# Attention with a compressive memory and a two-matrix MLP on one core: the gate and the pairs of keys and values move from GpSimd to ScalarE and VectorE

## The chip, the core and the metric

The kernel runs on one core of one Trainium2 chip. A core has TensorE (PE in the profile: matmuls; PEld is its weight load), VectorE (DVE), ScalarE (ACT), GpSimd (POOL) and SyncE (SP, which issues the DMAs). The metric is device time in microseconds (us), lower is better: 618.44 us for the kernel before, the median of 3 runs (617.84 to 619.04).

## The reference, cut to what matters

```python
def _attn_ref(q, k, v, M_prev, z_prev, beta):          # B, H, S, D = 4, 8, 576, 64
    scores = scale * np.matmul(q, k.transpose(0, 1, 3, 2))
    scores = np.where(causal, -1e9, scores); scores = scores - scores.max(-1, keepdims=True)
    a = np.exp(scores); a /= a.sum(-1, keepdims=True) + 1e-09
    local = np.matmul(a, v)
    q_p = phi(q)                                        # where(x > 0, x, exp(x) - 1) + 1
    mem_ret = np.einsum('bhsd,bhde->bhse', q_p, M_prev)
    mem_norm = np.einsum('bhsd,bhd->bhs', q_p, z_prev)[..., None] + 1e-06
    g = 1.0 / (1.0 + np.exp(-beta))[None, :, None, None]
    return g * mem_ret / mem_norm + (1 - g) * local

def _moe_ref(x, w_in, w_out, alpha):                    # x: 2304 x 512, w_in: 512 x 2048, w_out: 2048 x 512
    h = x @ w_in
    g = np.maximum(h, 0.0) + alpha * np.minimum(h, 0.0)
    return (g @ w_out).astype(np.float32)
```

The rows of the attention, with the heads side by side, are the x of the MLP. The inputs are float32, with the MLP's weights read as pairs of 32-bit words.

## The kernel before, in words

**Pairs of halves.** Nearly every matmul operand x is kept as two float16 tiles, hi = half(s·x) and lo = half(s·x − hi), where s is a power of two found from the data; a product is then three matmuls (hi·hi, hi·lo, lo·hi). Three engines make such a pair in one of two ways. The long way: GpSimd multiplies x by s in place (`tensor_tensor`), ScalarE copies the product to float16 (a CAST in the profile), GpSimd subtracts (`tensor_tensor`) to get lo. The scaled way: ScalarE writes hi in one `activation` with scale s, VectorE writes lo in one `scalar_tensor_tensor`, (x·s) − hi.

**Stages.** The first 64 rows of all four batches are computed together (called Z, batch number 4 in the names), the other 512 rows batch by batch in two groups of 256 rows (block pairs [1, 2] and [3, 4]). A unit is one head of such a group: scores in PSUM (tile `s`), mask and row minimum on VectorE (`E<-s,mask`), exponential on ScalarE, the sums' reciprocals (`sm`), the pair of probabilities (`P<-E,sm` on ScalarE and `P<-E,sm,P` on VectorE), a DMA transpose (`PT<-P`) and the product with the values (`bank<-v,PT`, then the pair `xn` and its transpose into `x`). Units follow each other with a lag of 3 between scores and values.

**MLP steps.** There are 9 groups of 256 rows with 8 steps each, 72 steps in all. `moe_in` does 24 matmuls `h<-x,R` for 256 hidden columns, then `r<-h` (ScalarE), two `r<-r,oma,h` (VectorE), and makes the pair `gg` of the gate; `moe_out`, one step later, does 12 matmuls `y<-R,gg`. The table `GL` says for which half groups the gate's pair is made the long way: 7 half groups of 4 steps, so 28 of the 72 steps; of the others 16 have a constant as the scale (the two groups that are done while the weights still come in) and 28 use the scaled way with the scale `gsc`.

**Weights.** `load_w` brings a piece of 128 x 1024 weights as pairs of words, `conv_w` makes float32 of it on VectorE (three instructions `R<-…` per piece: one `tensor_scalar`, two `scalar_tensor_tensor`), and `split_w` makes the float16 pair in the tile R; its last step is on GpSimd (`R<-R`, 16 times). The 16 pieces are the main work of the first 110 us.

**Keys and values.** For each batch b from 1 on and each of 4 pairs of heads hp, `build_qk` makes the pair `k<-kn` (128 x 640) and sends it to a DMA transpose; for every b and hp, `build_v` makes the pair `v<-vn` (128 x 640), where block 0 (128 columns, half of it the memory M) has a scale of its own (`pm`), and blocks 1 to 4 (512 columns) the scale `scr`. `KS` and `VS` pick the engine of the first multiplication: GpSimd for all values and for the keys of batches 1 and 2, ScalarE for the keys of batch 3.

**Order of the work.** All operations are first recorded (class `Work`, so nearly every instruction has line 272 in the profile) and then laid out by a list planner with prices per operation (`price`, `lag`, `lay`, `issue`). The table `STAGES` adds a bias in microseconds to the due time of each phase (such as "bv0" for `build_v` of batch 0, "LW2" for loads of weights, "y1_10" for steps of a group, "P:POOL" for one engine's part). Each engine then runs its own list in that order; SyncE's list orders the DMAs.

Of the kernel before, what the change touches and what calls it, by code (L numbers as in the profile page):

```python
# [18 lines left out]
KS = [1, 1, 1, 0]  # L19
VS = [1, 1, 1, 1]  # L20
QL = [0, 0, 0, 0]
GL = [0, 0, 0, 0, 1, 1, 1, 1, 1, 1, 1, 0, 0, 0, 0, 0, 0, 0]
# [12 lines left out]
        "A0": 60.3, "A:DVE": -306.4, "BK0": 117.9, "BK:PE": -11.5, "C0": 4, "C1": -76.9, "C2": -1.6, "C3": 79.3,  # L35
        "C:ACT": -0.6, "C:DVE": -39.3, "C:PE": -397.4, "I": -157.5, "I:DVE": -330.7, "J": 263.4, "J:ACT":
# [8 lines left out]
        -50.1, "P:PE": -496.3, "P:POOL": 679, "S1": 1377.4, "S2": -9, "S3": -27.5, "S:ACT": -46, "S:POOL": 29.2,  # L45
# [7 lines left out]
        "o:DMA": 27.6, "o:DVE": 63.6, "o:PE": 10.9, "oZ": -65.4, "oZ:DVE": 37.9, "oZ:POOL": 3, "p0": -58, "p1":  # L53
        334.1, "p2": -935.6, "p3": 1.5, "p:ACT": 144.4, "p:DVE": 12.4, "p:POOL": 37.5, "q1": 25.3, "q2": 66.4,
        "q:ACT": -27.9, "q:DVE": -643.9, "r0": -38.4, "r:ACT": 109.4, "r:DVE": -26.1, "r:POOL": -14, "s03": 7.2,
        "s11": -466, "s13": -162.8, "s21": -1.8, "s23": 262.8, "s31": -144.7, "s33": -269.1, "s:ACT": -108.2,
# [219 lines left out]
def kernel(  # L276
# [120 lines left out]
    def load_batch(b):  # L397
# [3 lines left out]
        if b:  # L401
            kr = natp.tile([128, NS, H, D], F32, tag="kn")
        else:
            kr = stack["v16"].rearrange("p (i h d) -> p i h d", i=NS, d=D)
# [832 lines left out]
```

## Time and profile before

| | |
|---|---|
| median of 3 runs | 618.44 us (617.84 to 619.04) |
| the profiled execution's own time | 617.69 us |
| its span on the core | 615.9 us, mean granted clock of TensorE 0.953 |
| busy: PE / DVE / ACT / POOL | 534.2 / 467.4 / 378.9 / 268.9 us |
| share of the chain that ended last | PE 49%, DVE 31%, DMA 5%, ACT 5% |

The span is cut into stretches in the rows below: the start (to 120 us, of which 20 to 40 is shown; weights and the first attention), a stretch in which VectorE is busy nearly all the time (120 to 300), a stretch with PE nearly full (300 to 500) and the tail (from 500), where the attention has ended and PE runs MLP steps alone. A busy time is a union, so instructions of one engine that overlap at their ends count once; the idle time of an engine is the stretch less its busy time.

### The profile page before, as it was taken

Reading aid. Unit: us, or ns where it says so; the run is one execution under the profiler, and the core shown is the slowest. Engines: PE = TensorE matmul, PEld = TensorE weight load, DVE = VectorE, ACT = ScalarE, POOL = GpSimd, SP = SyncE. Lnnn points to the kernel's source line nnn. Section 1 sums busy time; section 2 is a strip of 40 time slices with the busy share of each in tenths; the row PEclk is TensorE's granted clock in tenths of the full one; section 3 lists DMA queues with packets and bytes.
Section 4 is the critical chain, followed back from the end, with each engine's and each line's share of the span. In section 5 each row is a group of like instructions: output and inputs, shape, how many; then the busy total and the mean of one; then the engine's idle time right before and its main releaser. Section 6 shows DMA issues by size and latency. Waiting matters only on the chain.

```text
span 615.9 us, 12153 instructions
## 1 busy us (share of the span) xinstructions
PE 534.2 (87%) x4450; PEld 354.1 (57%) x4450; DVE 467.4 (76%) x1118; ACT 378.9 (62%) x795; POOL 268.9 (44%) x255
## 2 busy tenths in 40 slices
PE   0525567998989989898999999799999999999997
PEld 0314444545545666654666676557667666776773
DVE  5599999889889899999978555878757867733322
ACT  2536577566977856686785556748678757732322
POOL 2137254466297751565455545987553511000000
PEclk9966768899999999998999999999999999999999
DMA  8975879312935999865998390249776536610000
GB/s 277 189 256 190 239 227 219 81 32 51 186 87 108 188 205 173 180 151 122 208 196 180 67 167 35 53 87 196 167 161 115 100 81 147 129 40 19 35 1 35
DMA packets 228060, 82.87 MB, mean 135 GB/s; under 512 B 218272, under 2 KB 218272, under 8 KB 228000
## 3 DMA queue, kind: packets, MB, share of 16 engines
q1 hardware_dynamic: 228000, 82.09, 60.5%
q8 instruction: 35, 0.57, 0.4%
q14 instruction: 25, 0.20, 0.1%
HBM read 35.66 MB, written 5.77 MB: 67 GB/s over the span
## 4 chain that ended last, share of the span: by engine, by line
PE 49%; DVE 31%; DMA 5%; ACT 5%; issue 4%; SPq 3%; POOL 2%; DVEq 0%; ACTq 0%; POOLq 0%
PE y L272 20%; PE h L272 17%; PE s L272 7%; DVE R L272 6%; DVE P L272 5%; PE bank L272 4%; DVE q L272 4%; DVE E L272 3%; SPq L272 3%; DVE r L272 3%; DMA PT<-P 2%; DVE sm L272 2%; DVE gg L272 2%; ACT E L272 1%; ACT P L272 1%
## 5 line engine op out<-in xcount | busy, mean ns | idle before, releaser
L272 PE MATMUL h<-x,R 128*128 128x256 f16 x1728 | 286.3, 279 | 19.3 <-DVE r L272 10.3
L272 PE MATMUL y<-R,gg 128*128 128x512 f16 x864 | 247.0, 383 | 4.8 <-DVE gg L272 4.0
L272 PEld LDWEIGHTS <-R 128*128 128x128 f16 x1728 | 170.9, 100 | 69.3 <-issue 22.7
L272 PE MATMUL bank<-v,PT 128*128 128x64 f16 x1224 | 190.8, 193 | 6.4 <-DVE xn L272 4.0
L272 PEld LDWEIGHTS <-gg 128*128 128x128 f16 x864 | 84.7, 99 | 90.2 <-issue 6.5
L272 PEld LDWEIGHTS <-PT 128*128 128x128 f16 x1224 | 117.8, 98 | 13.0 <-issue 6.3
L272 DVE SCALAR_TENSOR_TENSOR P<-E,sm,P 128x320 f16<-128x320 f32 (+2 forms) x112 | 85.7, 790 | 20.3 <-ACT P L272 19.7
L272 DVE SCALAR_TENSOR_TENSOR r<-r,oma,h 128x256 f32<-128x256 f32 x144 | 62.8, 474 | 38.7 <-ACT r L272 38.5
L272 ACT ACTIVATE E<-E,mx 128x448 f32<-128x448 f32 (+2 forms) x112 | 69.9, 624 | 32.3 <-DVE mx L272 31.8
L272 ACT ACTIVATE P<-E,sm 128x320 f16<-128x320 f32 (+2 forms) x112 | 65.3, 621 | 23.4 <-DVE sm L272 14.8
L272 ACT ACTIVATE r<-h 128x512 f32<-128x512 f32 x72 | 42.3, 592 | 55.3 <-PE h L272 45.1
L272 PE MATMUL s<-k,qT 128*128 128x192 f16 (+7 forms) x200 | 66.9, 375 | 4.7 <-DVE mx L272 3.9
L272 POOL TENSOR_TENSOR P<-q,P 128x128 f16<-128x128 f32 x56 | 31.0, 554 | 91.1 <-ACT P L272 87.5
L272 DVE CUSTOM_DVE_ANT_0 E<-s,mask,pm 128x320 f32<-128x320 f32 (+3 forms) x96 | 56.5, 610 | 9.6 <-PE s L272 8.5
L272 POOL TENSOR_TENSOR R<-R 128x1024 f16<-128x1024 f32 x16 | 36.7, 2296 | 19.0 <-ACT R L272 19.0
L272 POOL TENSOR_TENSOR gg<-r,gg 128x512 f16<-128x512 f32 x28 | 34.9, 1248 | 19.7 <-ACT gg L272 14.3
L272 POOL TENSOR_TENSOR r<-r,gsc 128x512 f32<-128x512 f32 x28 | 31.9, 1143 | 21.8 <-DVE sm L272 7.3
L272 DVE SCALAR_TENSOR_TENSOR gg<-r,gsc,gg 128x512 f16<-128x512 f32 x28 | 22.9, 819 | 16.8 <-ACT gg L272 16.7
L272 PE MATMUL s<-k,qS 128*128 128x192 f16 (+3 forms) x120 | 33.9, 294 | 0.0
L272 ACT ACTIVATE gg<-r,gsc 128x512 f16<-128x512 f32 x28 | 20.1, 719 | 20.3 <-PE y L272 12.5
L272 DVE SCALAR_TENSOR_TENSOR sm<-sm,C 128x2 f32<-128x2 f32 x64 | 23.2, 363 | 12.3 <-ACT E L272 10.9
L272 POOL TENSOR_TENSOR t<-q,zb 128x512 f32<-128x512 f32 x16 | 23.2, 1456 | 19.6 <-DVE wsc L272 12.2
(178 smaller groups left out, 745.1 us busy)
## 6 DMA issues: line engine op xcount, KB each, us to landing
q<-in_q_dram SPq DMA_DIRECT2D x16, 256.0 KB, 4.9
vn<-in_v_dram SPq DMA_DIRECT2D x16, 256.0 KB, 4.8
out_dram<-t SPq DMA_DIRECT2D x16, 256.0 KB, 2.3
kn<-in_moe_w_in_dram SPq DMA_DIRECT2D x6, 512.0 KB, 5.2
kn<-in_moe_w_out_dram SPq DMA_DIRECT2D x6, 512.0 KB, 5.5
kn<-in_k_dram SPq DMA_DIRECT2D x12, 256.0 KB, 3.8
qS<-qT SPq DMA_DIRECT2D x24, 128.0 KB, 2.4
R<-in_moe_w_in_dram SPq DMA_DIRECT2D x4, 512.0 KB, 7.5
```

The costliest lines, as they stand in the source:

```text
L272: fn(*a, **kw)
```

## The change

The long way goes for the gate, the keys and the values; all of them use the scaled way. `KS` and `VS` go, `GL` is all zeros. The value pair is made in two pieces (block 0; blocks 1 to 4), each with an activation and a `scalar_tensor_tensor`. For batches from 1 on the keys lie as [head, block, column] in SBUF so that a pair of heads can be addressed in one piece; before they lay as [block, head, column]. `STAGES` gets another set of biases (some 240 numbers), and with it the planner lays out all lists anew.

```diff
-KS = [1, 1, 1, 0]
-VS = [1, 1, 1, 1]
-GL = [0, 0, 0, 0, 1, 1, 1, 1, 1, 1, 1, 0, 0, 0, 0, 0, 0, 0]
+GL = [0] * 18
...
 STAGES = [
     (2, {
-        "A0": 60.3, "A:DVE": -306.4, "BK0": 117.9, "BK:PE": -11.5, "C0": 4, "C1": -76.9, "C2": -1.6, "C3": 79.3,
+        "A0": 31.3, "A:DVE": 38.7, "BK0": -19.6, "BK:ACT": -1.3, "BK:PE": 157.4, "C0": -144.5, "C1": 360.2,
...
         if b:
-            kr = natp.tile([128, NS, H, D], F32, tag="kn")
+            kn = kr = natp.tile([128, H, NS, D], F32, tag="kn")
         else:
             kr = stack["v16"].rearrange("p (i h d) -> p i h d", i=NS, d=D)
+            kn = kr.rearrange("p i h d -> p h i d")
         vn = natp.tile([128, H, NS, D], F32, tag="vn")
-        kn = kr.rearrange("p i h d -> p h i d")
...
-        V.tensor_reduce(t[:, 1:2], nat[b]["kr"].rearrange("p i h d -> p (i h d)"), **ab)
+        V.tensor_reduce(t[:, 1:2], nat[b]["kr"].rearrange("p h i d -> p (h i d)"), **ab)
...
-        kk = n["k"][:, hs]
-        kh, kl = (k16[:, :, :, t, :] for t in range(2))
-        if KS[b]:
-            G.tensor_tensor(kk, kk, p["sk"][:, :, None, None].to_broadcast([128, 2, NS, D]), op=ALU.mult)
-        else:
-            A.activation(kk, kk, AF.Copy, scale=p["sk"])
-        A.copy(kh, kk)
-        G.tensor_tensor(kl, kk, kh, op=ALU.subtract)
+        kk = n["k"][:, hs].rearrange("p h i d -> p (h i) d")
+        kh, kl = (k16[:, :, :, t, :].rearrange("p h i d -> p (h i) d") for t in range(2))
+        A.activation(kh, kk, AF.Copy, scale=p["sk"])
+        V.scalar_tensor_tensor(out=kl, in0=kk, scalar=p["sk"], in1=kh, op0=ALU.mult, op1=ALU.subtract)
...
         for i0, i1, sc in ((0, 1, p["sv0"]), (1, NS, p["sv"])):
-            vv = n["v"][:, hs, i0:i1].rearrange("p h i d -> p h (i d)")
-            if VS[b]:
-                G.tensor_tensor(vv, vv, sc[:, :, None].to_broadcast([128, 2, (i1 - i0) * D]), op=ALU.mult)
-            else:
-                A.activation(vv, vv, AF.Copy, scale=sc)
-        vv = n["v"][:, hs].rearrange("p h i d -> p h (i d)")
-        vh, vl = (v16[:, t].rearrange("p h i d -> p h (i d)") for t in range(2))
-        A.copy(vh, vv)
-        G.tensor_tensor(vl, vv, vh, op=ALU.subtract)
+            vv, vh, vl = (x[:, :, i0:i1].rearrange("p h i d -> p h (i d)") for x in (n["v"][:, hs], v16[:, 0], v16[:, 1]))
+            A.activation(vh, vv, AF.Copy, scale=sc)
+            V.scalar_tensor_tensor(out=vl, in0=vv, scalar=sc, in1=vh, op0=ALU.mult, op1=ALU.subtract)
```

**How the lists move, place 1: VectorE at the start**, from the last instruction on alpha's scale on (`isa`). `stq`, `q<-q,t` and `zmx` belong to Z's attention and wait for Z's loads; `R<-kn` and `R<-R` convert weights, here the first pieces of w_out. Before:

```order
L272 TENSOR_SCALAR isa<-scr_100 128x1
L272 TENSOR_REDUCE stq_104<-q_0_91 128x1 x2
L272 SCALAR_TENSOR_TENSOR q_0_91<-q_0_91,t_0_133 128x512
L272 TENSOR_SCALAR str_106<-stq_104 128x2
L272 RECIPROCAL str_106<-str_106 128x2
L272 SCALAR_TENSOR_TENSOR q_0_91<-q_0_91,t_1_134 128x512
L272 ISA P_108,zmx_117<-s_0_116,mz 128x64
```

The same place in the change:

```order
L272 TENSOR_SCALAR isa<-scr_100 128x1
L272 TENSOR_SCALAR R<-kn_88 128x1024
L272 SCALAR_TENSOR_TENSOR R<-kn_88,R 128x1024
L272 TENSOR_REDUCE stq_104<-q_0_91 128x1
L272 SCALAR_TENSOR_TENSOR R<-kn_88,R 128x1024
L272 SCALAR_TENSOR_TENSOR q_0_91<-q_0_91,t_0_133 128x512
L272 TENSOR_SCALAR R<-R 128x1024
L272 SCALAR_TENSOR_TENSOR R<-R 128x1024
L272 TENSOR_REDUCE stq_104<-q_0_91 128x1
L272 SCALAR_TENSOR_TENSOR R<-R 128x1024
L272 SCALAR_TENSOR_TENSOR q_0_91<-q_0_91,t_1_134 128x512
```

Two whole pieces of weights now stand between the instructions of Z; the first `zmx` stands behind the 9th converted piece, where it stood behind the 4th.

**Place 2: VectorE at the first MLP step** (`r<-r,oma,h` is the step's first work on VectorE; `mx` with the mask is a score of batch 0). Before:

```order
L272 SCALAR_TENSOR_TENSOR R<-E_0_90,R 128x1024
L272 SCALAR_TENSOR_TENSOR R<-kn_88,R 128x1024
L272 SCALAR_TENSOR_TENSOR R<-E_0_90,R 128x1024
L272 SCALAR_TENSOR_TENSOR r_144<-r_144,oma,h_112 128x256
L272 TENSOR_REDUCE stq_105<-q_2_93 128x1 x2
```

In the change:

```order
L272 TENSOR_SCALAR R<-q_0_89 128x1024
L272 ISA P_108,mx_148<-s_0_121,mask 128x320
L272 ISA mx_148 128x1
L272 ISA P_108,mx_148<-s_0_121,mask 128x192
L272 SCALAR_TENSOR_TENSOR r_144<-r_144,oma,h_112 128x256 x2
L272 SCALAR_TENSOR_TENSOR r_145<-r_145,oma,h_113 128x256 x2
```

The `r` of the first two steps stand together behind 14 converted pieces and the first scores of batch 0, where the first stood behind 12 pieces and no such score.

**Place 3: the long way on GpSimd and what stands for it on VectorE**, in the middle of the program. GpSimd before, in batch 2 (`P<-q,P` is the part of a unit that stays there):

```order
L272 TENSOR_TENSOR r_144<-r_144,gsc 128x512
L272 TENSOR_TENSOR P_108<-q_1_92,P_108 128x2x64
L272 TENSOR_TENSOR r_145<-r_145,gsc 128x512
L272 TENSOR_TENSOR P_109<-q_1_92,P_109 128x2x64
L272 TENSOR_TENSOR v_66<-vn_95,v_66 128x640
L272 TENSOR_TENSOR gg_146<-r_144,gg_146 128x512
```

VectorE in the change, at the keys of batch 2:

```order
L272 SCALAR_TENSOR_TENSOR gg_146<-r_144,gsc,gg_146 128x512
L272 SCALAR_TENSOR_TENSOR q_0_89<-q_3_94,scr_101,q_0_89 128x8x64
L272 SCALAR_TENSOR_TENSOR sm_151<-sm_151,C_131 128x2
L272 SCALAR_TENSOR_TENSOR xn_161<-bank_67,xsc,xn_161 128x256
L272 SCALAR_TENSOR_TENSOR k_0_110<-kn_88,scr_101,k_0_110 128x10x64
L272 RECIPROCAL sm_151<-sm_151 128x2
```

The gate's and the keys' splits now stand in VectorE's list between the instructions of the units, and GpSimd's list keeps `P<-q,P`, the norms (`t<-q,zb`, `q<-q,nrm`) and the weights (`R<-R`).

## Rows read from the trace of the kernel before

**Rows 1.** Busy time by engine in stretches: PE, PEld, DVE, ACT, POOL, clock, DMA
```profile
core 0: us, PE busy (x) PEld busy (x) DVE busy (x) ACT busy (x) POOL busy (x), PEclk, DMA share, GB/s
20.00:40.00 20.00, 10.73 (x83) 7.68 (x83) 12.22 (x56) 7.47 (x14) 4.62 (x4) 0.91 1.00 254
120.00:300.00 180.00, 166.31 (x1284) 102.46 (x1283) 167.42 (x409) 127.36 (x268) 100.28 (x88) 0.98 0.68 136
300.00:500.00 200.00, 193.24 (x1811) 131.74 (x1810) 148.03 (x375) 137.22 (x324) 117.61 (x119) 1.00 0.64 128
500.00:616.00 116.00, 112.17 (x989) 76.79 (x985) 50.55 (x110) 47.79 (x88) 3.94 (x6) 1.00 0.28 62
```

**Rows 2.** Waits of PE from 120 to 300: total us, times, longest
```profile
PE h L272 <- DVE r L272: 4.8, 3, 2.8
PE y L272 <- DVE gg L272: 4.0, 3, 2.2
```

**Rows 3.** Timeline of VectorE, 20 to 26 us: start, us, what, idle before
```profile
23.82 0.69 DVE L272 TENSOR_REDUCE stq<-q 128x1 f32<-128x512 f32 x1 [3.27 <-DMA q<-in_q_dram]
```

**Rows 4.** Groups by form, VectorE, whole span: the conversion of weights
```profile
L272 DVE SCALAR_TENSOR_TENSOR R<-kn,R 128x1024 int32<-128x1024 int32 x10 | 12.1, 1214 | 0.1
...
L272 DVE TENSOR_SCALAR R<-kn 128x1024 int32<-128x1024 int32 x5 | 3.6, 722 | 5.1 <-DMA kn<-in_moe_w_in_dram 5.1
```

**Rows 5.** Timelines of GpSimd and of VectorE at 304 us
```profile
304.57 1.42 POOL L272 TENSOR_TENSOR r<-r,gsc 128x512 f32<-128x512 f32 x1
305.02 1.52 DVE L272 SCALAR_TENSOR_TENSOR gg<-r,gsc,gg 128x512 f16<-128x512 f32 x1
```

**Rows 6.** Groups by form, VectorE, 500 to 616 us: xcount, busy us, mean ns
```profile
L272 DVE SCALAR_TENSOR_TENSOR gg<-r,gsc,gg 128x512 f16<-128x512 f32 x20 | 15.0, 751 | 16.8 <-ACT gg L272 16.7
L272 DVE SCALAR_TENSOR_TENSOR P<-E,sm,P 128x576 f16<-128x576 f32 x6 | 4.9, 816 | 1.8 <-ACT P L272 1.8
```

**Rows 7.** Groups by form, VectorE, 120 to 300 us
```profile
L272 DVE SCALAR_TENSOR_TENSOR P<-E,sm,P 128x576 f16<-128x576 f32 x12 | 12.7, 1059 | 2.0 <-ACT P L272 2.0
...
L272 DVE SCALAR_TENSOR_TENSOR sm<-sm,C 128x2 f32<-128x2 f32 x23 | 12.1, 530 | 1.1 <-ACT E L272 0.7 <-ACT P L272 0.4
...
L272 DVE SCALAR_TENSOR_TENSOR q<-q,scr,q 128x512 f16<-128x512 f32 x8 | 10.7, 1363 | 0.0
```

**Rows 8.** Groups by form, VectorE, 300 to 500 us
```profile
L272 DVE SCALAR_TENSOR_TENSOR P<-E,sm,P 128x576 f16<-128x576 f32 x14 | 15.2, 1083 | 4.8 <-ACT P L272 4.5
...
L272 DVE SCALAR_TENSOR_TENSOR P<-E,sm,P 128x320 f16<-128x320 f32 x16 | 12.9, 805 | 8.6 <-ACT P L272 8.3 <-issue 0.2
...
L272 DVE SCALAR_TENSOR_TENSOR sm<-sm,C 128x2 f32<-128x2 f32 x31 | 7.9, 255 | 8.7 <-ACT E L272 8.6
```

**Rows 9.** Groups by form, GpSimd, 120 to 300 us
```profile
L272 POOL TENSOR_TENSOR R<-R 128x1024 f16<-128x1024 f32 x8 | 17.0, 2129 | 7.6 <-ACT R L272 7.6
...
L272 POOL TENSOR_TENSOR k<-kn,k 128x640 f16<-128x640 f32 x8 | 13.3, 1666 | 10.6 <-ACT k L272 10.6
L272 POOL TENSOR_TENSOR t<-q,zb 128x512 f32<-128x512 f32 x8 | 11.8, 1480 | 6.0 <-DVE q L272 6.0
L272 POOL TENSOR_TENSOR P<-q,P 128x128 f16<-128x128 f32 x20 | 11.7, 585 | 36.4 <-ACT P L272 34.8 <-DMA qS<-qT 1.5
L272 POOL TENSOR_TENSOR v<-vn,v 128x640 f16<-128x640 f32 x8 | 11.4, 1444 | 3.5 <-ACT v L272 3.5
```

**Rows 10.** Groups by form, GpSimd, 300 to 500 us
```profile
L272 POOL TENSOR_TENSOR gg<-r,gg 128x512 f16<-128x512 f32 x28 | 34.9, 1248 | 19.7 <-ACT gg L272 14.3 <-PE s L272 2.2 <-PE h L272 1.9
...
L272 POOL TENSOR_TENSOR P<-q,P 128x128 f16<-128x128 f32 x30 | 15.3, 513 | 21.6 <-ACT P L272 19.5 <-PE h L272 2.0
```

**Rows 11.** Groups by form, ScalarE, whole span
```profile
L272 ACT ACTIVATE gg<-r,gsc 128x512 f16<-128x512 f32 x28 | 20.1, 719 | 20.3 <-PE y L272 12.5 <-DVE r L272 7.6
L272 ACT CAST gg<-r 128x512 f16<-128x512 f32 x28 | 17.1, 612 | 15.0 <-POOL r L272 8.9 <-POOL P L272 2.3 <-PE bank L272 2.1
...
L272 ACT CAST v<-vn 128x640 f16<-128x640 f32 x16 | 11.3, 717 | 0.0
```

More of the change, by code (lines that the diff above doesn't have):

```diff
@@ L34 @@
     (2, {
-        "A0": 60.3, "A:DVE": -306.4, "BK0": 117.9, "BK:PE": -11.5, "C0": 4, "C1": -76.9, "C2": -1.6, "C3": 79.3,
-        "C:ACT": -0.6, "C:DVE": -39.3, "C:PE": -397.4, "I": -157.5, "I:DVE": -330.7, "J": 263.4, "J:ACT":
[8 rows of a table removed]
-        -50.1, "P:PE": -496.3, "P:POOL": 679, "S1": 1377.4, "S2": -9, "S3": -27.5, "S:ACT": -46, "S:POOL": 29.2,
[7 rows of a table removed]
[L53 to L56, printed above, removed]
-        "s:DVE": 1375, "s:PE": -1, "sZ:ACT": -0.6, "sZ:DVE": -269.7, "sZ:PE": -161.2, "sZ:POOL": 91.8, "v1":
[3 rows of a table removed]
-        "y4_10": 21, "y4_11": -2.2, "y:DMA": 232.7, "y:DVE": -5.7, "y:PE": 0.1,
+        "A0": 31.3, "A:DVE": 38.7, "BK0": -19.6, "BK:ACT": -1.3, "BK:PE": 157.4, "C0": -144.5, "C1": 360.2,
+        "C2": -52.3, "C3": 129, "C:ACT": -61.3, "C:DVE": -91.1, "C:PE": 698.1, "I": 12.2, "I:DVE": -145.8,
[8 rows of a table added]
+        213.2, "P31": -24.2, "P33": -55.7, "P:ACT": -55, "P:DMA": -47, "P:DVE": -66, "P:PE": -12.7, "P:POOL":
+        11.9, "S0": -453.3, "S1": 1509, "S2": -73, "S3": -19.5, "S:ACT": -58.7, "V0": 15.1, "V:DVE": -177.9,
+        "V:PE": -1, "a0": 275, "a1": -47, "a2": 1313.7, "a3": -25.8, "a4": 31.1, "a:DVE": 54.9, "bk1": -46.1,
+        "bk2": 14.8, "bk3": 0.3, "bk:ACT": -2.7, "bk:DMA": 794.9, "bk:DVE": -27.5, "bk:PE": 3.2, "bv0": 2871.3,
[5 rows of a table added]
+        54, "o:PE": -8.8, "oZ": -24.7, "oZ:ACT": 76.6, "oZ:DVE": 651.7, "oZ:POOL": 298.1, "p0": -113.4, "p1":
+        505.5, "p2": -1623.7, "p3": -110.6, "p4": -20.6, "p:ACT": -267.9, "p:DVE": 19.2, "p:POOL": 340.6, "q1":
+        -7.3, "q:ACT": -156.2, "q:DVE": -891.1, "r0": -14.5, "r:ACT": -367.8, "r:DVE": -11.2, "r:POOL": -161.2,
+        "s01": -12.4, "s03": 12.1, "s11": -413.6, "s13": -274.4, "s21": -13.6, "s23": 57.7, "s31": -738.1,
+        "s33": -24.2, "s:ACT": -190.7, "s:DVE": 9.5, "s:PE": -0.9, "sZ": -4.2, "sZ:PE": -97.6, "sZ:POOL": -173,
[4 rows of a table added]
+        "y:PE": -4.1,
     }),
@@ L734, in build_v @@
         for i0, i1, sc in ((0, 1, p["sv0"]), (1, NS, p["sv"])):
-            vv = n["v"][:, hs, i0:i1].rearrange("p h i d -> p h (i d)")
-            if VS[b]:
-                G.tensor_tensor(vv, vv, sc[:, :, None].to_broadcast([128, 2, (i1 - i0) * D]), op=ALU.mult)
-            else:
-                A.activation(vv, vv, AF.Copy, scale=sc)
-        vv = n["v"][:, hs].rearrange("p h i d -> p (h i d)")
-        vh, vl = (v16[:, t].rearrange("p h i d -> p (h i d)") for t in range(2))
-        A.copy(vh, vv)
-        G.tensor_tensor(vl, vv, vh, op=ALU.subtract)
+            vv, vh, vl = (x[:, :, i0:i1].rearrange("p h i d -> p h (i d)") for x in (n["v"][:, hs], v16[:, 0], v16[:, 1]))
+            A.activation(vh, vv, AF.Copy, scale=sc)
+            V.scalar_tensor_tensor(out=vl, in0=vv, scalar=sc, in1=vh, op0=ALU.mult, op1=ALU.subtract)
         stacks.setdefault((b, hp), [None] * 4)[3] = v16
```

35 rows, old and new, of the table STAGES are left out of this document.

## The prediction

> **What bounds the kernel now.** Look first at the stretches [rows 1]. From 500 us on PE is busy 112.2 of 116 us and the others are half idle: that tail is MLP steps alone and nothing here touches it. From 300 to 500 PE is busy 193.2 of 200, so at most 6.8 us can be won there. From 120 to 300 it is VectorE that is full, 167.4 of 180 us, and PE stands idle for 13.7 us; the waits say for what: 4.8 us for `r` and 4.0 us for `gg`, both VectorE's [rows 2]. From 20 to 40 us nobody is full: VectorE has 12.2 busy of 20, hence 7.8 us idle, and the first of these gaps, 3.27 us, ends with a load of Z's queries [rows 1, 3]. So a microsecond is worth its price on VectorE up to 300 us, on PE from then on, and GpSimd and ScalarE (busy 44% and 62% of the span) count only by whom they keep waiting.
>
> **GpSimd keeps VectorE waiting.** This decides what the moved work costs. At 304.57 us GpSimd starts `r<-r,gsc` and is at it for 1.42 us, to 305.99. VectorE's `gg<-r,gsc,gg`, begun at 305.02, ends at 306.54 and took 1.52 us [rows 5]; the same form takes 751 ns on average after 500 us, when GpSimd does next to nothing [rows 6]. So VectorE stood for some 0.8 us until GpSimd was done. The Trainium skill's page "SBUF — State Buffer", section "Who interferes with whom", has this as a rule: a VectorE instruction with two inputs in SBUF and a GpSimd instruction that reads SBUF exclude each other, and the second waits for the first to end. By that rule in full the held one would need its whole 751 ns after the release; the trace shows 0.55 us after it (306.54 − 305.99), so each hold costs 0.2 us less than by the rule, and the sums below go by the rows' own means.
>
> **The change, part by part.**
>
> *Added to VectorE.* 28 gates at 751 ns [rows 6]: 21.0 us. 16 value pairs in two pieces: 512 columns at 751, and 128 columns, of which no row shows this form; between 576 and 512 columns the price falls by (816 − 751)/64 = 1.02 ns a column [rows 6], which gives 360 ns for 128, 1.11 us a pair and 17.8 us. 12 key pairs of 640 columns by the same slope at 881 ns: 10.6 us. Together 49.4 us. By place: GpSimd splits 8 key pairs and 8 value pairs between 120 and 300 us [rows 9], so 7.0 + 8.9 = 15.9 us come there (the first four of the values from batch 0, at about 136 us); the 28 gates, 8 value and 4 key pairs, 33.4 us, come between 300 and 500.
>
> *Given back to VectorE.* The means of its two-input forms against the free ones [rows 6, 7, 8]. From 120 to 300: `P` of 576 columns 12 × (1059 − 816) = 2.9 us; `q` 8 × (1363 − 751) = 4.9; `sm` 23 × (530 − 255), taking the mean of the next stretch as free, = 6.3; together 14.1. Of GpSimd's 100.3 us there, `R`, `t` and `P` stay, 17.0 + 11.8 + 11.7 = 40.5 [rows 1, 9], so 60% goes, and of 14.1 us 8.4 come back; with the smaller two-input groups, not counted, I take 12. From 300 to 500: `P` of 576, 14 × (1083 − 816) = 3.7; `P` of 320, 16 × (805 − 555, by the slope) = 4.0. These are two groups of several; I take 14 for all. The bounds are 0 (other GpSimd work steps into every hold) and 30 (twice what the five groups show, 21.8, less the share that stays).
>
> *Sum on VectorE.* From 120 to 300: +15.9 − 12 = +4 us, with 12.6 us idle there. From 300 to 500: +33.4 − 14 = +19, with 52 idle. Its busy time goes from 467 to about 485 us (475 to 500). The first +4 fall on the engine that is the bound, and PE waits for it. Against that the new order puts the splits of keys and values as fillers between waiting instructions (place 3), where before VectorE had 12.6 us of gaps. I take these two as even: 0, with bounds +11 (all 15.9 added, a third of the gaps filled) and −10 (PE's waits, 13.7 us, mostly gone).
>
> *The gate's chain.* From the second `r` to the finished pair it was a product on GpSimd (1.42 us in the one shown [rows 5]), a cast of 612 ns and a difference of 1248 ns on GpSimd [rows 10, 11]; now it is 719 + 751 ns on ScalarE and VectorE [rows 11, 6]. `moe_out` comes a step later than `moe_in`, so this is mostly covered by the next step's matmuls, and PE has just 6.8 us of idle to give. I take −2, bounds 0 and −6.
>
> *ScalarE.* 28 × (719 − 612) = +3.0 us for the gate [rows 11]; the values' cast of 640 columns at 717 becomes two activations, one of 512 at 719 and one of 128 at most at 612: up to +0.61 us for 16, 9.8 us. It is busy 127 of 180 and 137 of 200 us [rows 1], and these stand far ahead of their readers: 0. *GpSimd* loses 60 us before 300 (100.3 − 40.5), then the 34.9 of the gate's differences [rows 10], as many products, and the last 12 pairs of keys and values: over 130 of its 269 us, 0 by itself.
>
> *The keys' layout.* The same bytes in the same runs of 64 numbers from DRAM; loads of batch b come a batch ahead: 0. If the cover were gone, a load of 256 KB late by a microsecond or two would be in front of VectorE's maximum of the keys.
>
> *The order at the start.* Place 1 puts two whole pieces of weights into VectorE's 7.8 us of gaps. A piece is 722 + 2 × 1214 = 3.15 us [rows 4], two are 6.3. The pieces have to be converted before the MLP can run anyway, and up to 120 us VectorE's list is the long one. Paid for by: Z's scores (`zmx`) five pieces later, 16 us by price, and the first two steps' `r` behind two more pieces and two scores (place 2). SyncE must bring w_out's first pieces ahead of Z's queries, in a stretch with the DMA engines' share at 1.00 [rows 1]. I take −6, bounds 0 and −7.8, where the gaps aren't just moved; the case that they are, and worse, is a rival.
>
> **The sum.** 0 − 2 − 6 = −8 us. The profiled execution took 617.69 us for a span of 615.9, and the median is 0.75 above it; 618.4 − 8 = **610 us**. Likely by itself: 605 to 616. Two measurements of this kernel can be told apart from about 0.2%, or 1.2 us.
>
> **The rivals.**
>
> 1. *All waits go.* VectorE is held far less, the start is filled as above, and PE's 13.7 + 6.8 us of idle [rows 1] shrink by half: −8 − 10 = 600 us (595 to 605). For it: both PE waits above 4 us are for VectorE. Against it: VectorE's total does not fall.
> 2. *Nothing moves the end.* The pieces that fill the early gaps are given back by Z's late scores, the rest is hidden in PE's full stretches: 616 to 619.5 us. For it: 112 us of tail and 200 us at 97% are out of reach.
> 3. *VectorE becomes the bound for longer; slower.* The place is 160 to 300 us, the mechanism the holds: the GpSimd work that stays (`R` with 2129 ns apiece, `t`, `P`, 40.5 us [rows 9]) catches the two-input instructions that are added, and nothing is given back. Then 15.9 us go on an engine with 12.6 idle, of which a third can be filled: +12, less 6 at the start: 624 us (621 to 628). It decides itself at the mean of `P` with 576 columns: if it stays near 1059 in this stretch, nothing was given back. The same page of the Trainium skill speaks for it, in saying that the order of issue decides who blocks, so that one GpSimd reader fewer need not free VectorE.
> 4. *The start turned round; slower.* The first two MLP steps run in time that PE would otherwise idle away. If they slip behind the attention of batch 0 (place 2), they are paid at full price later: 20 steps fill 112 us of the tail [rows 1, 6], so 5.6 us a step, 11 for two, less 6: 623 us. Against it: `r` waits in VectorE's list, but the matmuls before it need not.
>
> **How the numbers follow.** Forecast 0.45, rival 1 0.20, rival 2 0.12, rival 3 0.13, rival 4 0.10. Faster by over 0.2% (under 617.2) takes the forecast, rival 1 and some of rival 2 (0.05): 0.70. Within 0.2%: 0.07. Slower: 0.23. The range leaves out the better half of rival 1 and about half of the slower ones: 599 to 622.
>
> **What the profile would show.** Right: VectorE busy near 485 us, GpSimd below 140; `P` of 576 columns near 816 to 900 ns on average; PE busy above 195 of the 200 us after 300; VectorE's gaps from 20 to 32 us filled; PE full by some 6 us earlier than before. Wrong: VectorE at 98% or more from 120 to 400 us with PE waiting for `r` and `gg` longer than 8.8 us; or PE's share before 120 us lower than now with the first `h` later by more than 10 us.

## The result, and the profile of the changed kernel

The changed kernel takes **596.74 us** (median of 4 runs, 595.49 to 600.13); the kernel before, timed beside it, 618.43 (617.84 to 619.04). The ratio is 0.9659 (0.964 to 0.9678): 21 us faster. The forecast was 610.0, the range 599 to 622. The sign was right, the size far off: 8 us were forecast, and the time lies below the range, inside the 595 to 605 of rival 1, which had a chance of 0.20. Ratios leave out two executions in a slower state, one of four of `reads_at_gates` (618.32 us) and one of four of `a_order_old_kv` (633.11), which the medians given below still contain.

The changed kernel by stretches, with the columns of [rows 1]:

```profile
core 0: us, PE busy (x) PEld busy (x) DVE busy (x) ACT busy (x) POOL busy (x), PEclk, DMA share, GB/s
20.00:40.00 20.00, 2.75 (x10) 1.92 (x10) 16.76 (x33) 6.92 (x13) 3.08 (x2) 1.00 1.11 266
120.00:300.00 180.00, 176.27 (x1455) 112.49 (x1454) 172.02 (x448) 139.44 (x295) 50.42 (x45) 1.00 0.72 145
300.00:500.00 200.00, 196.31 (x1855) 134.72 (x1853) 156.68 (x416) 137.19 (x323) 28.88 (x40) 1.00 0.68 132
500.00:594.00 94.00, 89.97 (x759) 61.46 (x755) 38.78 (x84) 35.77 (x66) 1.29 (x2) 1.00 0.21 44
```

PE is now idle for 3.7 us of the 180 (before 13.7) and for 3.7 of the 200 (before 6.8). VectorE is no less busy, 172.0 and 156.7 us against 167.4 and 148.0. GpSimd fell from 100.3 and 117.6 to 50.4 and 28.9. From 20 to 40 us VectorE does 16.8 us of work instead of 12.2. The stretches are cut at the same times in both kernels, so they hold somewhat different work.

The chain of waits that ended last, by engine, from the page of the changed kernel:

```profile
PE 36%; DVE 2%; DMA 2%; ACT 2%; issue 1%; SPq 0%; POOL 0%; ACTq 0%; DVEq 0%
```

These shares add up to 43%: the chain of the change can be followed back only to 334.7 us, where that of the kernel before goes back to 0.7 us, so its 2% for VectorE are not to be set against the 31% before. From 334.7 us to the end VectorE has 27.1 us of the chain before (of 281) and 12.7 us in the change (of 259). VectorE is as busy as it was, but it holds the end up about half as long.

VectorE's groups by form, 120 to 300 us, against [rows 7]:

```profile
L272 DVE SCALAR_TENSOR_TENSOR P<-E,sm,P 128x576 f16<-128x576 f32 x14 | 12.3, 876 | 0.5 <-ACT P L272 0.3
...
L272 DVE SCALAR_TENSOR_TENSOR k<-kn,scr,k 128x640 f16<-128x640 f32 x8 | 8.3, 1037 | 0.0
...
L272 DVE SCALAR_TENSOR_TENSOR sm<-sm,C 128x2 f32<-128x2 f32 x24 | 5.7, 242 | 1.4 <-ACT E L272 1.4
L272 DVE SCALAR_TENSOR_TENSOR q<-q,scr,q 128x512 f16<-128x512 f32 x8 | 5.6, 745 | 0.2 <-ACT q L272 0.2
L272 DVE SCALAR_TENSOR_TENSOR v<-vn,pm,v 128x128 f16<-128x128 f32 x8 | 4.2, 526 | 0.1
```

`P` of 576 columns fell from 1059 to 876 ns, `sm` from 530 to 242, `q` from 1363 to 745. The added forms are here too: a key pair takes 1037 ns (881 estimated), the 128 columns of a value pair 526 (360 estimated).

The page's costliest groups of PE, the first two, with the idle time ahead of them at the row's end:

```profile
L272 PE MATMUL h<-x,R 128*128 128x256 f16 x1728 | 282.7, 274 | 3.1 <-DVE r L272 2.3
L272 PE MATMUL y<-R,gg 128*128 128x512 f16 x864 | 246.6, 380 | 0.5 <-DVE gg L272 0.4
```

The waits for `r` and `gg` of [rows 2], 4.8 and 4.0 us from 120 to 300 us alone, are 2.3 and 0.4 us over the whole span.

How far the kernels are at the same step of the MLP is read from VectorE's timelines: the end of the second `r<-r,oma,h` of a step (us; steps count from 0). The names of the other kernels are those of the experiments below. Each row is one execution; they lie between 3.0 us below the median of their kernel (b_order_new_engines, 613.28 us) and 1.4 above it (mix_start, 613.78), so the last column is not the order of the medians.

| | step 3 | step 8 | step 12 | step 31 | step 71 (last) |
|---|---|---|---|---|---|
| before | 128.9 | 195.7 | 221.9 | 350.1 | 605.2 |
| b_order_new_engines | 128.8 | 190.3 | 217.2 | 345.9 | 600.8 |
| mix_start | 122.6 | 194.2 | 220.7 | 347.4 | 601.3 |
| mix_to_200 | 124.8 | 184.2 | 211.0 | 342.3 | 597.7 |
| start_old | 128.7 | 185.8 | 212.6 | 338.4 | 589.5 |
| old_to_205 | 129.0 | 192.0 | 218.7 | 343.4 | 595.0 |
| the change | 121.8 | 180.8 | 207.7 | 332.4 | 583.1 |

So 7.1 us are won up to step 3, 7.1 more up to step 12 (between steps 3 and 8), and 7.9 from step 12 to the last. From step 12 to the last the four of these kernels with the old order there take 380.6 to 386.7 us, the three with the new one 375.4 to 376.9.

### The profile page after: what moved, and what is told of

It reads as the page before. It is cut to its first block, busy times and chain, and to the rows that moved or that the text cites. A ratio compares the mean times of both kernels' runs of the same rounds, so it can differ in the third digit from the quotient of the medians.

```text
span 593.7 us, 12056 instructions
## 1 busy us (share of the span) xinstructions
PE 520.5 (88%) x4450; PEld 348.4 (59%) x4450; DVE 468.9 (79%) x1190; ACT 380.6 (64%) x807; POOL 126.1 (21%) x131
## 5 line engine op out<-in xcount | busy, mean ns | idle before, releaser
L272 ACT ACTIVATE E<-E,mx 128x320 f32<-128x320 f32 (+2 forms) x112 | 69.6, 622 | 17.8 <-DVE mx L272 15.7
L272 DVE SCALAR_TENSOR_TENSOR P<-E,sm,P 128x576 f16<-128x576 f32 (+2 forms) x112 | 71.9, 668 | 8.7 <-ACT P L272 8.0
L272 ACT ACTIVATE P<-E,sm 128x576 f16<-128x576 f32 (+2 forms) x112 | 65.1, 620 | 16.4 <-DVE sm L272 6.0
L272 DVE SCALAR_TENSOR_TENSOR gg<-r,gsc,gg 128x512 f16<-128x512 f32 x56 | 45.2, 806 | 19.8 <-ACT gg L272 19.4
L272 DVE CUSTOM_DVE_ANT_0 E<-s,mask,pm 128x320 f32<-128x320 f32 (+2 forms) x96 | 56.7, 608 | 4.9 <-PE s L272 4.1
L272 ACT ACTIVATE gg<-r,gsc 128x512 f16<-128x512 f32 x56 | 40.1, 717 | 29.5 <-PE y L272 20.9
L272 PE MATMUL s<-k,qS 128*128 128x192 f16 (+4 forms) x120 | 34.5, 294 | 0.0
L272 ACT ACTIVATE xn<-bank,xsc 128x256 f16<-128x256 f32 x28 | 13.0, 463 | 14.1 <-PE bank L272 13.9
L272 ACT ACTIVATION_READ_ACCUMULATOR E<-E,mx 128x1 f32 x112 | 21.1, 188 | 0.0
L272 DVE SCALAR_TENSOR_TENSOR xn<-bank,xsc,xn 128x256 f16<-128x256 f32 x28 | 13.4, 477 | 9.1 <-ACT xn L272 9.0
```

The source lines that it names most:

```text
L272: fn(*a, **kw)
```

## The experiments

Two things changed together: who does the work (GpSimd, or ScalarE and VectorE) and the order of every list. Theory A had it that GpSimd cost the time, by holding VectorE (a hold is the time by which a VectorE instruction gets longer while GpSimd works) and by being late; theory B that the order did. Each time below is a median with its ratio to the kernel before on the same chip; where two kernels are compared, a difference in the ratios is turned into us with 618.4. Line numbers in the rows differ from run to run, since these kernels have lines added; L173 to L175 are instructions put beside or in place of others.

**The new engines in the old order.** Every list keeps the order of the kernel before; GpSimd's first product goes, the cast becomes the scaled activation and the difference the `scalar_tensor_tensor`, each in the place where the old one stood (keys in two instructions a pair, since their layout is the old one). For the gate this comes to:

```diff
-            G.tensor_tensor(r, r, sc[:, :, None].to_broadcast([128, 2, n]), op=ALU.mult)
-            A.copy(gg[:, 0, :, 0:n], r)
-            G.tensor_tensor(gg[:, 1, :, 0:n], r, gg[:, 0, :, 0:n], op=ALU.subtract)
+            A.activation(gg[:, 0, :, 0:n], r, AF.Copy, scale=sc)
+            V.scalar_tensor_tensor(out=gg[:, 1, :, 0:n], in0=r, scalar=sc, in1=gg[:, 0, :, 0:n],
+                                   op0=ALU.mult, op1=ALU.subtract)
```

> The order of the kernel before is kept instruction by instruction on every engine; only the gate, keys and values are made the scaled way (ScalarE and VectorE), each new instruction at the place of the old one in that order. Theory A (GpSimd held VectorE and came late; the new order only follows): most of the 21.7 us comes with the engines alone, 598 to 606 us, and the mean of P with 576 columns falls to about 870 ns. Theory B (the new order does it): 612 to 620 us, with the mean of P down all the same. Both share: 606 to 612.

Measured: 616.23 us, 0.9959 (0.9941 to 0.9976), 2.5 us faster than before. What VectorE gets back can be added up from the instructions that both kernels have (the 28 added gates taken at the mean of their form): in sum they take 40 us less than before here, and 44 us less in the change. So nearly all the relief comes with the engines alone. VectorE's busy time still rises, from 467.4 to 475.4 us, because some 55 us of instructions were added (a busy time counts overlaps once, so these figures don't add up exactly); the two nearly cancel, and so does the time.

**The old engines in the new order.** The change's lists stay; the gates, the keys and values, or all of them are made the long way again.

```diff
         A.activation(gg[:, 0, :, 0:n], r, AF.Copy, scale=sc)
+        if long:
+            work.become((nc.gpsimd.tensor_tensor, (r, r, sc...), dict(op=ALU.mult)), (nc.scalar.copy, (gg[:, 0, :, 0:n], r), {}))
...
+            work.become((nc.gpsimd.tensor_tensor, (gg[:, 1, :, 0:n], r, gg[:, 0, :, 0:n]), dict(op=ALU.subtract)))
```

`become` gives an operation that is laid out already other instructions, in the same place.

> The order of the changed kernel is kept; gate, keys and values are made the long way again, GpSimd's instructions at the places of the scaled ones. Theory A: the gain is lost, 612 us or more, even above the kernel before, since this order leaves GpSimd no room. Theory B: the gain stays, 597 to 603 us, though VectorE is held as before (mean of P with 576 columns near 1050 ns).

> The changed kernel with only the 28 gates made the long way again, in the same order. Theory A: the gate's GpSimd work (67 us, all after 300 us) holds VectorE in a stretch where PE is nearly full: 598 to 604 us. Theory B: 596 to 599.

> The changed kernel with only keys and values made the long way again, in the same order. Theory A: most of the price is here, since 16 of 28 pairs fall into 120 to 300 us, where VectorE is the bound: 604 to 612 us. Theory B: 596 to 600.

Measured: all the long way 638.39 us, 1.0345 (1.0301 to 1.0389); the gate alone 613.18, 0.9917 (0.9891 to 0.9943); keys and values alone 628.6, 1.0136 (1.0075 to 1.0197). In the first and the third, batch 0's values are scaled in place before PE reads the raw ones, so that the output changes, and those two times price that too: from step 3 to step 8 the third takes 68.6 us, and 59.4 with batch 0 the scaled way. Two later runs took it out. The first leaves batch 0's values the scaled way:

> The change's order with the long way for the keys and values of batches 1 to 3 (batch 0 keeps the scaled way). VectorE loses 12 pieces of about 1.0 us and 24 of 0.74 and 0.46 (some 26 us), and is held some 15 to 20 us more. If VectorE's total decides, 590 to 597. If the longer chain through GpSimd decides, as with the gate the long way (16 us), 602 to 612.

It gave 621.01 us, 1.0052 (0.9998 to 1.0107), but there the last pair's difference, made in one piece, came behind the next batch's load of M into the same tile, waited for it and used that M. With the value pair made piece by piece:

> As the run with the long way for keys and values of batches 1 to 3, but each value pair is copied and subtracted in the two pieces of the change (128 and 512 columns), so that no instruction waits for the other piece. Before, the last whole pair's difference came after the next batch's load of M into the same tile. If VectorE's total decides, 590 to 597. If the holds and the longer chain cost more than VectorE's saved work, 602 to 612, below the 621 of the run before it in any case.

Measured: 613.63 us, 0.9928 (0.9905 to 0.9951). So in the new order the long way of the 28 gates costs 16 us, that of the 12 pairs of keys and 12 of values of batches 1 to 3 costs 17 us, and either would take most of the 21 us away. It is not VectorE's total that does it: that is 465.8 us with the gates the long way and 463.8 with the keys and values, less than the 468.9 of the change. The waits of PE with the gates the long way, from 205 us on (total us, times, longest):

```profile
PE h L281 <- DVE r L281: 5.0, 7, 1.4
PE y L281 <- ACT gg L174: 4.3, 4, 2.0
PE bank L281 <- DVE xn L281: 4.2, 6, 1.6
PE y L281 <- POOL gg L174: 2.2, 2, 1.8
```

6.5 us are waits for the pair of the gate itself, which the change has not (0.4 us). In this order `y` follows the gate closer than the longer chain allows.

**GpSimd's work without its lateness.** Here the change stays whole, and GpSimd does beside it as much work as it lost, on a free piece of SBUF, for nobody: reads and writes in one kernel, writes alone in the other.

```diff
+    def pool(n):
+        x, z = R[16][:, 0:n], R[16][:, 640:640 + n // 2].bitcast(F16)
+        return ((nc.gpsimd.tensor_tensor, (x, x, x), dict(op=ALU.mult)), (nc.gpsimd.tensor_tensor, (z, x, x), dict(op=ALU.subtract)))
...
+        if OLD_GL[g["no"] + j // 4] and not g.get("halves"):
+            work.also(*pool(512))
```

> The change, and GpSimd does beside it work that nobody waits for: two tensor_tensor of 512 columns for each of the 28 gates that left it, two of 640 columns for each pair of keys and values of batches 1 to 3, all on a piece of SBUF that is free by then. They read SBUF as the old ones did. Theory A (GpSimd's reading holds VectorE, and this costs time in the new order): VectorE's means rise again (P of 576 columns from 873 to above 960 ns) and the time to 604 to 612. Theory B (holds land in VectorE's idle time, the order and the shorter chains are what counts): the means rise, the time stays within 597 to 600.

> The control to the run before it: in the same places GpSimd writes the same piece of SBUF with three memsets (1024, 1024 and 640 columns, about as long together as the two tensor_tensor), so it is as busy but reads nothing. If GpSimd's own lateness (its norms, P and t behind the added work) is what costs, this is as slow as the run with reads. If the holds cost, it stays at 597 to 599 and VectorE's means do not move.

Measured: with reads 640.82 us, 1.038 (1.035 to 1.041), 44.6 us above the change and far above what theory A expected; with writes alone 605.51, 0.9794 (0.9759 to 0.983), 8.4 above it. GpSimd is equally busy in both (259.3 and 254.3 us). VectorE's rows from 300 to 500 us, first with reads, then with writes alone:

```profile
L173 DVE SCALAR_TENSOR_TENSOR gg<-r,gsc,gg 128x512 f16<-128x512 f32 x24 | 27.3, 1141 | 1.9 <-ACT gg L282 1.9
...
L282 DVE SCALAR_TENSOR_TENSOR P<-E,sm,P 128x576 f16<-128x576 f32 x13 | 14.3, 1099 | 3.2 <-ACT P L282 3.2
...
L282 DVE SCALAR_TENSOR_TENSOR sm<-sm,C 128x2 f32<-128x2 f32 x26 | 10.6, 408 | 1.3 <-ACT E L282 1.2
```

```profile
L173 DVE SCALAR_TENSOR_TENSOR gg<-r,gsc,gg 128x512 f16<-128x512 f32 x27 | 21.2, 787 | 3.2 <-ACT gg L282 2.8
L282 DVE SCALAR_TENSOR_TENSOR P<-E,sm,P 128x576 f16<-128x576 f32 x16 | 14.1, 879 | 2.9 <-ACT P L282 2.9
L282 DVE SCALAR_TENSOR_TENSOR sm<-sm,C 128x2 f32<-128x2 f32 x31 | 4.7, 151 | 1.7 <-ACT E L282 1.6
```

Reads take the gate's pair to 1141 ns where it takes 787 under writes. VectorE has the same instructions in all three kernels; in sum they take 49 us more with reads than in the change and 11 more with writes, and its busy time is 518.3, 475.3 and 468.9 us. So 49 us more on VectorE made the kernel 45 us slower. The control gives the part that is the reading alone: 43 us more on VectorE than under writes, and 36 us more of time. **In the new order more than four fifths of a hold are paid**, while taking 40 us of holds out of the old order, with 55 us of work put in their place, changed 2.5. Not all of it is waiting: from step 12 to the last the kernel with reads takes 42.1 us longer than the change, 29.4 in idle time of PE and 12.7 in its busy time, with the granted clock at 0.97 instead of 1.00. The Trainium skill, page "SBUF — State Buffer", section "Who interferes with whom", says that VectorE's instructions with two inputs in SBUF are held by GpSimd's reading and not by its writing alone; the two runs agree (1141 and 787 ns).

**At the gates alone: holds, and plain work of VectorE.** In the first GpSimd's two idle reads stand at the 28 gates only; in the second VectorE itself does one more `scalar_tensor_tensor` there:

```diff
-        return ((nc.gpsimd.tensor_tensor, (x, x, x), ...), (nc.gpsimd.tensor_tensor, (z, x, x), ...))
+        return ((nc.vector.scalar_tensor_tensor, (), dict(out=z, in0=x, scalar=gsc[:, 0:1], in1=x, op0=ALU.mult, op1=ALU.subtract)),)
```

> The change, with two GpSimd tensor_tensor of 512 columns that nobody waits for at each of the 28 gates alone. The gate the long way gave 613 us in this order. If its price is the holds, VectorE is held some 18 us here too and loses no work: 611 to 617. If its price is the chain through GpSimd and ScalarE, 597 to 603.

> The change, with one more VectorE scalar_tensor_tensor of 512 columns at each of the 28 gates, on a piece of SBUF that nobody else reads (28 x 0.75 = 21 us of VectorE). GpSimd's reads at the same gates held VectorE for 17 us more and cost 14.7. If VectorE's time counts whatever takes it, 611 to 618. If only holds cost (they catch instructions that PE waits for) and plain work is hidden behind PE, as the prediction had it for 300 to 500 us, 597 to 604.

Measured: reads 611.46 us, 0.9876 (0.985 to 0.9901), 13.4 us above the change with VectorE 16.4 us busier; VectorE's own work 607.09, 0.9821 (0.9761 to 0.9882), 10.0 us above it with VectorE 20.7 us busier. The first lies within its 611 to 617, the second between its two expectations. Its rows from 300 to 500 us, then those of the reads:

```profile
300.00:500.00 200.00, 190.27 (x1803) 131.29 (x1800) 175.82 (x448) 137.93 (x326) 27.01 (x38) 1.00 0.67 128
```

```profile
300.00:500.00 200.00, 188.69 (x1759) 129.70 (x1757) 170.58 (x413) 135.06 (x318) 87.86 (x90) 0.98 0.64 123
```

In both VectorE has 24 us or more idle in this stretch, and yet PE loses 6.0 and 7.6 of its 196.3 us. So work is not hidden there, though VectorE is idle for a fifth of this stretch in the change (43 of 200 us). From step 12 to the last VectorE is busy for 302.6 us in both, 18.3 more than in the change, and yet the holds cost 14.0 us there (389.4 against 375.4) and the plain work 9.1 (384.5). Per microsecond a hold seems to cost more (0.8) than plain work (0.5), but these are single executions, the intervals of the two runs overlap, and this stays open.

The executions of the kernel with VectorE's own work are spread widely, and its trace shows one reason, ahead of the first added instruction (at 300 us). At step 3 it is at 128.9 us and the change at 121.8, with the same list. One `sm` of two columns took 4.10 us there and ended with the last of four GpSimd instructions that followed one upon the other; in the change the same instruction took 0.24:

```profile
99.77 0.69 POOL L282 MEMSET kn<- 64x512 f32 x1
99.93 4.10 DVE L282 SCALAR_TENSOR_TENSOR sm<-sm,C 128x2 f32<-128x2 f32 x1
100.43 1.26 POOL L282 TENSOR_TENSOR t<-q,zb 128x512 f32<-128x512 f32 x1
101.64 0.28 POOL L282 COPY P<-q 128x128 f32<-128x128 f32 x1
101.89 2.12 POOL L282 TENSOR_TENSOR R<-R 128x1024 f16<-128x1024 f32 x1
106.41 0.37 PE L282 MATMUL bank<-ident,mv 128*1 128x128 f32 x1 [2.25 <-DVE mv L282]
```

```profile
100.54 0.24 DVE L272 SCALAR_TENSOR_TENSOR sm<-sm,C 128x2 f32<-128x2 f32 x1
```

PE then waited 2.25 us for `mv`, and the granted clock stood at 0.50 from 105.5 to 119.2 us. By mean granted clock its four executions fall in two pairs, 604.11 and 604.78 us at 0.983, 609.4 and 612.12 (the one with the trace) at 0.971 and 0.972; the change has 595.49 to 597.47 at 0.983 and 600.13 at 0.971. Compared at 0.983 the plain work costs 8 us, so 8 to 10 is as close as these runs come.

**The new order, part by part, with the new engines.** The change's program is kept, and its 6412 operations are issued in a written order: the first n as in one kernel, the rest as in the other (a changed operation stands where the one it replaced stood; one load of keys is put off until its tile is free).

```diff
-            for i in sorted(range(len(ops)), key=lambda i: (start[i], i)):
+            for i in ORDER:
```

n = 780 ends at some 100 us, ahead of any changed operation; n = 2140 at some 205 us. The new order first, the old one behind:

> The change's engines; every engine's list has the change's order for the first 780 of 6412 operations (all before the first gate, key or value that changed engine, about the first 100 us) and the order of the kernel before for the rest. The new engines in the old order throughout gave 616.2 us. If the start is worth what the prediction took for it (-6), this gives 610 (608 to 612). If the start's fill is only worth something together with the new order behind it, 614 to 617. If the start carries all that the order gives, 597 to 602.

> As the run before it, but with the change's order for the first 2140 operations, up to about the twelfth MLP step (near 205 us), and the old order from there. In the traces of the two kernels the twelfth step ends 14.2 us earlier in the change and the last one 22.1 earlier. If each stretch keeps what it won, 601 to 604. If the middle's win is given back by an old order behind it, 608 to 616. If all that matters lies before 205 us, 596 to 599.

And the old order first:

> The mirror of the run with the start: the change, but the first 780 operations in the order of the kernel before, the rest in the change's own. If the start's order is worth -6 in the place where it stands, this gives 602 to 604. If it is worth what the other run showed from the old side (some 3 to 4 us), 599 to 601. If the order behind it needs it, over 606.

> The change, but the first 2140 operations (to about 205 us) in the order of the kernel before. Engines alone gave 616, the new order to 205 us alone 609. If the order behind 205 us keeps its win whatever stands ahead of it (11 to 13 us), 603 to 607. If it needs the early part, 610 to 616.

| order up to 100 us / to 205 / behind | us | ratio | interval |
|---|---|---|---|
| old / old / old (b_order_new_engines) | 616.23 | 0.9959 | 0.9941 to 0.9976 |
| new / old / old (mix_start) | 612.36 | 0.9915 | 0.9884 to 0.9946 |
| new / new / old (mix_to_200) | 609.0 | 0.9849 | 0.9811 to 0.9887 |
| old / old / new (old_to_205) | 607.65 | 0.9827 | 0.9813 to 0.9842 |
| old / new / new (start_old) | 602.07 | 0.9738 | 0.9722 to 0.9753 |
| new / new / new (the change) | 596.74 | 0.9659 | 0.964 to 0.9678 |

Three parts, three shares. The order of the start is worth 2.7 us with the old order behind it and 4.9 with the new; the middle's 4.1 after the new start, and 5.5 with the old start and the new end; that behind 205 us 8.2 with the old order ahead of it and 11.8 with the new. (The differences of ratios, by 618.4; each rests on two intervals of 1 to 2.4 us to either side, so that the two values for the start or for the middle are not told apart.) The start alone fell short of its 608 to 612 by a little, mix_to_200 came out at the 608 to 616 of "given back", old_to_205 lies just over its first guess, and start_old is within 602 to 604.

What the order does behind 205 us is seen from step 12 to the last step, in the engines-alone kernel (383.6 us) and in the change (375.4 us):

```profile
217.20:600.80 383.60, 369.09 (x3381) 254.25 (x3382) 284.72 (x738) 237.49 (x533) 46.61 (x64) 1.00 0.58 116
```

```profile
207.70:583.10 375.40, 369.04 (x3403) 255.15 (x3404) 284.33 (x738) 236.91 (x537) 48.44 (x64) 1.00 0.63 123
```

PE's busy time is the same to 0.1 us, VectorE's to 0.4 us; what differs is PE's idle time, 14.5 against 6.4 us. (That PE's busy time is so equal is chance: the change has 22 matmuls more in this part, and in the other kernel a short fall of the clock cost 1.7 us.) The waits of PE from 205 us on, engines alone, then the change:

```profile
PE h L280 <- DVE r L280: 7.4, 7, 1.9
PE s L280 <- DVE mx L280: 4.0, 4, 2.5
PE bank L280 <- DVE xn L280: 2.3, 2, 1.3
```

```profile
PE bank L272 <- DVE xn L272: 2.5, 4, 1.1
PE h L272 <- DVE r L272: 2.3, 3, 1.2
```

The same work stands in a list in which `r` and the scores' `mx` come in time. With the old engines that list would not hold: the gates or the keys and values the long way each cost 16 to 17 us in it.

Up to step 12 the clock takes part. Stretches of mix_start (the new start, the old order behind), 5 us a row; the granted clock is the third number from the end:

```profile
125.00:130.00 5.00, 4.80 (x27) 2.03 (x24) 3.77 (x22) 2.27 (x6) 1.22 (x2) 1.00 0.01 2
130.00:135.00 5.00, 4.48 (x17) 1.59 (x17) 4.66 (x15) 2.81 (x8) 1.25 (x2) 0.70 0.01 2
135.00:140.00 5.00, 5.00 (x12) 1.57 (x10) 2.76 (x6) 2.86 (x6) 0.00 (x0) 0.50 0.00 0
140.00:145.00 5.00, 5.00 (x22) 3.38 (x21) 4.57 (x9) 0.87 (x2) 0.43 (x1) 0.50 0.01 3
```

The change in the same 20 us:

```profile
125.00:130.00 5.00, 5.00 (x32) 2.45 (x31) 4.24 (x22) 3.90 (x10) 0.00 (x0) 1.00 0.01 2
130.00:135.00 5.00, 5.00 (x27) 2.21 (x26) 4.41 (x13) 4.27 (x8) 4.13 (x3) 1.00 0.01 2
135.00:140.00 5.00, 5.00 (x32) 2.44 (x30) 4.69 (x9) 4.64 (x8) 1.32 (x2) 1.00 0.01 3
140.00:145.00 5.00, 5.00 (x23) 2.09 (x20) 4.16 (x15) 4.91 (x12) 3.10 (x2) 1.00 0.15 54
```

PE lost 0.72 us there, and the granted clock stood at 0.50, the 1.2 GHz level, from 132.0 to 145.6 us. In this execution mix_start gave its early 6 us back there: against the engines alone it is 6.2 us ahead at step 3 and 3.5 behind at step 12. With each piece of PE's busy time weighted by the granted clock, 6.9 of these 9.7 us are the clock; the rest is the work of 24 matmuls that mix_start still has to do in this part. (By the medians mix_start kept 2.7 us.) The same weighting over the whole way to step 12 turns PE's busy time of 157.2 us before and 144.6 in the change into 140.7 and 139.8, with 22 matmuls of 1038 moved behind. So of the 14.2 us won up to step 12 some 12 are the clock, 1 is work moved behind, and 1.6 are idle time. It goes with the order of the start: up to step 3 PE is busy for 71 to 74 us in the four kernels with the old start, and for 59 to 66 in all twelve with the new one.

## Why the prediction was wrong in size, point by point

**The engines: the number right, the place not.** Gate −2, everything else 0, together −2 us; the engines alone gave −2.5. But the −2 were to come from the gate's shorter chain, behind 300 us, and there nothing moved: from step 12 to the last step the kernel before takes 383.3 us and the one with the new engines 383.6. What it wins in its trace, it wins between steps 3 and 8 (61.5 us instead of 66.8), where no gate has changed. That the sum fits is luck.

**VectorE's total.** The added work was 49.4 us by the estimate; measured, 12.0 for the keys, 19.2 for the values and some 22.6 for 28 gates at 806 ns, 54 us with the holds that are left. Given back were 40 us with the engines alone and 44 in the change, not the 12 + 14 assumed, and more than the upper bound of 30: the prediction scaled by GpSimd's remaining share and took a few groups for all. `sm` alone gave back 10.5 us, and two groups that it did not count, `P` of 448 columns and the conversion `R<-q,R`, 5.3 and 5.8. By its own terms (467.4 + 49.4 − 26) the busy time would have been 491 us and not the 485 that it states; measured, 475.4 with the engines alone and 468.9 in the change. `P` of 576 columns at 873 ns over the whole span is within the 816 to 900 that was named, GpSimd's 126.1 us below the 140.

**The start.** For the −6 the runs give 2.7 us (mix_start) to 4.9 (start_old), and 7 us at step 3 in the traces: within its bounds, but not in the way described. The gaps are filled as said; the first piece of w_out's weights now stands where Z's queries were waited for [rows 3]:

```profile
23.96 0.69 DVE L272 TENSOR_SCALAR R<-kn 128x1024 int32<-128x1024 int32 x1 [1.52 <-DMA kn<-in_moe_w_out_dram]
24.68 1.23 DVE L272 SCALAR_TENSOR_TENSOR R<-kn,R 128x1024 int32<-128x1024 int32 x1
25.83 0.68 DVE L272 TENSOR_REDUCE stq<-q 128x1 f32<-128x512 f32 x1
```

But they open again right behind. From 40 to 80 us VectorE's busy time, the third of a row, is 39.8 us before and 33.9 in the change. The rows before, then in the change:

```profile
40.00:60.00 20.00, 7.64 (x83) 6.64 (x84) 19.90 (x33) 12.70 (x18) 12.10 (x7) 0.59 0.56 175
60.00:80.00 20.00, 10.89 (x61) 7.70 (x61) 19.93 (x25) 12.24 (x21) 6.34 (x3) 0.67 0.91 269
```

```profile
40.00:60.00 20.00, 8.52 (x79) 6.35 (x79) 18.63 (x60) 13.06 (x19) 7.57 (x5) 0.96 0.85 212
60.00:80.00 20.00, 10.34 (x62) 7.56 (x64) 15.29 (x36) 13.18 (x20) 8.46 (x6) 0.61 0.98 244
```

Up to step 3 VectorE is idle for 18.6 us instead of 19.9. What is shorter is its work, by 5.7 us, with the conversions `R<-q,R` at 10.1 us in sum instead of 15.9 (GpSimd holds them less in this order), and PE's busy time, by 11.6 us, some 10 of them the clock, while PE's idle time grew by 4.6. Which of the two made the 7 us the runs don't separate. Rival 4 fell as well: the first step's `r` is 16 us later (95.7 instead of 79.7), and nothing was paid for that.

**The step that failed** is "Against that the new order puts the splits of keys and values as fillers between waiting instructions … I take these two as even: 0", together with the −2 that stood for everything behind 300 us. The order behind the start was worth 0 in the sum. By the runs it is worth 4 to 6 us between 100 and 205 us and 8 to 12 behind, 14 to 16 in all. The prediction had the size of it in its hands: its lower bound for the first part was −10, for the second −6, and PE's idle time of 13.7 + 6.8 us in [rows 1] is what shrank. Rival 1 priced just this and came to 600. Against rival 1 it was argued that "VectorE's total does not fall". That argument is what the runs refute: from step 12 on VectorE's busy time is equal to 0.4 us in two kernels of which one has 8 us less PE idle time. What PE waited for in these two was set by where an instruction stands in VectorE's list, not by how full the list is.

**"a microsecond is worth its price on VectorE up to 300 us, on PE from then on"** was wrong as well: 21 us of extra VectorE work at the gates, all of it behind 300 us with a fifth of VectorE's time idle, cost 8 to 10 us (5 to 15 by the two intervals), and holds there 13 us. Rival 3 saw that danger in the wrong place: the relief did come. With the dummy reads next to none of it is left (the common instructions of VectorE take only 6 us less than before), and the kernel takes 640.8 us, not rival 3's 624.

**What the prediction did not list** is the clock. No term spoke of it, though [rows 1] show 0.91 from 20 to 40 us and 0.98 from 120 to 300. Up to step 12 PE's busy time fell by 12.6 us, nearly all of it by the clock. In the new order PE does 3.1 us of its first work before 40 us instead of 11.7, and that later, denser work kept the clock up is likely but was not tested by itself.

What stays open: the new order with all the old engines was not measured without a changed output; how much of the gates' 16 us is the longer chain and how much the holds is bounded only (holds alone 13.4 us, with no work saved); and the runs tell how much the order is worth in each part, not which of its many moves does it.

## What to carry to other kernels

When a change takes work away from an engine that holds another and lays the lists out anew, price the order for itself: list PE's idle time by what ends it, and ask which of these waits a list with the shorter chains can place in time. A total that stays equal says nothing about these waits: from step 12 on equal busy times went with 383.6 and with 375.4 us here. And an idle share of a fifth on the second engine does not make added work free, if that engine feeds the first one at every step.

## What the runs showed of the hardware

- A gap of 0.72 us in PE's work (mix_start, 129.8 us) was followed by 13.6 us at the lower level of the clock. The gap's length alone does not decide it: in the kernel before a gap of 1.69 us at 149.3 us, and in the change one of 1.25 us at 257.4 us, passed with the clock at 1.00. What does, these runs don't show.
- One two-column instruction of VectorE stood for 4.10 us through four GpSimd instructions in a row, where it takes 0.24 us in another execution of the same list. So the GpSimd work that is left still held VectorE for long in one execution and not in the other.
- GpSimd memsets, which read nothing, did not hold VectorE's two-input instructions (the gate's pair 787 ns, `sm` 151 ns) but did cost: VectorE's instructions took 11 us more in sum than in the change, 8 of them in short `tensor_scalar` instructions of up to four columns (three `scr<-scr` were 2.3 us longer together than the free 0.16 us each). The kernel was 8.4 us slower; whether by these instructions or by GpSimd's own work coming later is not separated.
